# Contracting over 64 features at once in the last query groups of a fused attention and ELU kernel on Trainium2

## The chip, the core and the metric

The kernel runs on one core of a Trainium2 chip. A core has a matrix engine (PE, with its weight loads PEld), a vector engine (DVE), a scalar engine (ACT), a general engine (POOL) and a sync engine (SP) that issues most transfers. [...] The matrix engine can be split into tiles: a matmul of "32*32" uses 32 rows (the contracted features) and 32 columns (the outputs) of the array, so sixteen of them can be placed side by side; of "64*32" eight fit.

The metric is the device time of one execution in microseconds; lower is better. Before the change the median of 3 runs is 262.61 us (262.29 to 262.78).

## The reference

```python
def phi(x):                                   # 32 numbers of a token -> 64 features
    a = einsum('rd,bhsd->bhsr', S1, x); b = einsum('rd,bhsd->bhsr', S2, x)     # r = 8
    return einsum('bhsi,bhsj->bhsij', a, b).reshape(..., 64)
q_p, k_p = phi(q), phi(k)                     # batch 4, heads 4, seq 1088, head_dim 32
kv  = einsum('bhsf,bhsd->bhfd', k_p, v);  z = sum(k_p, axis=2)
num = einsum('bhsf,bhfd->bhsd', q_p, kv)
den = einsum('bhsf,bhf->bhs', q_p, z)[..., None] + 1e-06
x   = (num / den) as 4352 tokens x 128
h   = x @ w_in                                # 128 x 2048
g   = where(h > 0, h, exp(min(h, 0)) - 1)
out = g @ w_out                               # 2048 x 128
```

All arithmetic is float32. S1, S2, w_in and w_out arrive as float64 and are rounded in the kernel from raw word pairs.

## The kernel before

Tokens are cut into half tiles of 64 (`NH` = 68 of them) and these into nine groups: groups 0 to 7 have 512 tokens, group 8 has the last 256, one half tile of 64 for each batch. The feed-forward part runs over groups and over eight pairs of 128-wide slices of the hidden dimension (`cp`). One group with one `cp` is a step; the list `steps` (L970) holds 64 of them, and the loop at L1074 writes the instructions out by hand for each: `mm1` (h from x, `quarters`, L256), the ELU on ACT (`elu_a`, L827 and L829) and DVE (`elu_d`, L835), sums on POOL (`sums7`, L717 to L720) and the second matmul of the step two before (`mm2_seven`, L756). From step 30 on both matmuls use 128*64 tiles. Step 46 is group 5 with `cp` 6, step 62 group 7 with `cp` 6; group 8 is worked off in a tail loop behind them.

The attention part is threaded through these steps with `at`, `mid` and `late`, which name a step and a place in it. For queries, `q1` makes a and b (and the terms of den) for a unit of groups, `q2_den` and `q2_half` divide by den and form the 64 products of each token (`qp`), `q4` turns them in blocks of 32 by 32 on DVE (L651) into `qpT`, and `q5` (L661) multiplies them with kv, giving x for the unit in PSUM; `q5_out` (L672) copies it to SBUF on ACT as `xg`. Units here are 2, 3, (4, 5), (6, 7) and 8. `queries` (L674) runs `q5` of one unit and `q1` of the next in one step, on two `h` banks that the next step's `mm1` uses and two more: step 46 has `q5` of unit 6 (256 columns for each matmul) and `q1` of group 8 (64 columns), step 62 has `q5` of group 8 alone (64 columns).

After `q4`, the 32 rows of one row group w of the array hold one quarter of the unit's tokens (`quarter_of`), 32 of the 64 features at a time: half f=0 and half f=1 lie beside each other in the free dimension. So `q5` is called twice: with f=0 for four heads and four quarters (16 matmuls of 32*32, opening the sums), then `q1` (16 matmuls of 32*32), then f=1 (16 more, closing the sums). The stationary operand is `kvs[b]`: kv of batch b, with 32 features on the partitions, copied to all four row groups. It is written by `KT_out` (L438): DVE turns kv, SP writes it to a DRAM buffer `kvd` (L442) and reads it back four times (once for batch 0) into `kvs` (L445). Units 6 and 7 belong to batch 3; group 8 has one quarter of each batch.

SP works its transfers in order: loads at the start, the copies of `KT_out`, and 16 stores at the end of each group (L804). The raw buffer `raw_2` (L160) of the first two weight slices is not used after their rounding.

Of the kernel before, what the change touches and what calls it, by code (L numbers as in the profile page):

```python
# [12 lines left out]
F32 = mybir.dt.float32  # L13
# [14 lines left out]
def kernel(  # L28
# [21 lines left out]
    nc = tc.nc  # L50
    B, H, S, D = q.shape
    R = S1.shape[0]
    P = 128
# [10 lines left out]
    const = ctx.enter_context(tc.tile_pool(name="const", bufs=1))  # L64
    work = ctx.enter_context(tc.tile_pool(name="wk", bufs=2))
# [75 lines left out]
    wide = S1.dtype != F32  # L141
# [17 lines left out]
    if wide:  # L159
        raw_2 = const.tile([P, 2, 4 * P, 2], U32, name="raw")  # L160
# [163 lines left out]


    kvS = const.tile([P, H, D], F32, name="kvS")
    kvs = {b: const.tile([P, H, 2, D], F32, name=f"kvs{b}") for b in range(B)}
    dram = ctx.enter_context(tc.tile_pool(name="dram", bufs=1, space=bass.MemoryType.DRAM))
    kvd = {b: dram.tile([P, 2 * D], F32, name=f"kvd{b}")[:] for b in range(B)}
    kv_ps, feats, wzs, kf_ps = {}, {}, {}, []  # L330
# [107 lines left out]
    def KT_out(b):  # L438

        kt = work.tile([P, 2 * D], F32, name="kvt", tag="kvt")  # L440
        nc.vector.transpose(kt[:], kv_ps[b][:, :R * R])
        nc.sync.dma_start(kvd[b], kt[:])  # L442
        src = kvd[b].rearrange("(h p) x -> p h x", h=H)
        for w in range(4 if b else 1):
            nc.sync.dma_start(kvs[b][32 * w:32 * w + 32].rearrange("p h f d -> p h (f d)"), src)  # L445

    def ZC(b, ps):
        zl = work.tile([P, H * R], F32, name="zl", tag="zl")
        nc.scalar.copy(zl[:], ps[:, R * R:R * R + H * R])
        return zl  # L450
# [30 lines left out]
    abw, ans, qp, qpT, xg, xps = {}, {}, {}, {}, {}, {}  # L481
# [7 lines left out]
    def half_tile(g, k):  # L489
        return (g // 2, 8 * (g % 2) + k) if g < NQ - 1 else (k, NT - 1)  # L490
# [37 lines left out]
    un = {g: sum(qn[x] for x in gr) for g, gr in units.items()}  # L528

    def quarter_of(g, w):  # L530

        n = un[g] // 2
        return (*half_tile(g + n * w // 8, n * w % 8), n)

    def q1(g, ps, o, opened):
        for w in range(4):
            b, t, n = quarter_of(g, w)
            m, qs = 64 * n, qE[:, b:b + 1, :] if g == NQ - 1 and b < 2 else qT[b][:, t:t + n, :]
            qs = qs.rearrange("p t s -> p (t s)")
            if g == 2:  # L540
                m, qs = 2 * m, _ap(qs, [[8 * 64, 2], [1, m]])
            for r in range(4):
                rows = slice(32 * r, 32 * r + 32)
                nc.tensor.matmul(ps[r][32 * w:32 * w + 32, o:o + m], SWs[rows, b].rearrange("p x r -> p (x r)"),  # L544
                                 qs[rows], start=not opened, stop=True, skip_group_check=True,
                                 tile_position=(32 * r, 32 * w))
        abw[g] = ps, o
# [79 lines left out]
            nc.scalar.copy(to[:, w], xp[w][:, :256].rearrange("p (m s) -> p m s", s=P))  # L627


    def heads(g):  # L630
        return 2 if un[g] > 4 else H

    def q2_a(g, i):
        m = heads(g) * un[g]
        p = psum.tile([P, 512], F32, name="qa", tag="aux")
        ans[g, i] = p[:, :m * R].rearrange("p (m r) -> p m r", r=R)
        nc.scalar.copy(p[:, :m * R], ans[g][:, m * i:m * i + m].rearrange("p m r -> p (m r)"))

    def q2_half(g, i):
        m = heads(g) * un[g]  # L640
        r = slice(m * i, m * i + m)
        qp[g, i] = work.tile([P, 4 * H, R, R], F32, name="qp", tag="qp", bufs=2)
        a_, b_ = ans.pop((g, i)) if (g, i) in ans else ans[g][:, r], abw[g][:, r, :R]
        nc.vector.tensor_mul(qp[g, i][:, :m], _ap(a_, list(a_.ap[1:]) + [[0, R]]),
                             _ap(b_, [b_.ap[1], [0, R], b_.ap[2]]))

    def q4(g, i=0):

        m = heads(g) * un[g]
        qpT[g, i] = work.tile([P, 4 * H, 2, 32], F32, name="qpT", tag="qpT", bufs=2)  # L650
        nc.vector.transpose(qpT[g, i][:, :m].rearrange("p m f s -> p (m f s)"),  # L651
                            qp.pop((g, i))[:, :m].rearrange("p m i j -> p (m i j)"))

    def q5(g, ps, f):
        m4 = un[g]
        for r in range(4):
            i, o = divmod(m4 * r, heads(g) * un[g])
            for w in range(4):
                b, t, n = quarter_of(g, w)
                rows = slice(32 * w, 32 * w + 32)  # L660
                nc.tensor.matmul(ps[w][32 * r:32 * r + 32, :64 * n], kvs[b][rows, r, f, :],  # L661
                                 qpT[g, i][rows, o:o + 2 * n, f, :], start=(f == 0), stop=(f == 1),
                                 skip_group_check=True, tile_position=(32 * w, 32 * r))
        xps[g] = ps

    def q5_out(g, i=0):
# [7 lines left out]
    def queries(g5, g1, n):  # L674

        hs[steps[n]] = [psum.tile([P, 512], F32, name="h", tag="h", bufs=4) for c in range(2)]
        ps = hs[steps[n]] + [psum.tile([P, 512], F32, name="qps", tag="aux") for _ in range(2)]
        if g5 is not None:
            q5(g5, ps, 0)
        if g1 is not None:  # L680
            q1(g1, ps, 256 if g5 is not None else 0, g5 is not None)
        if g5 is not None:
            q5(g5, ps, 1)


# [297 lines left out]
    def late(n, f, *a):  # L983
        extra.setdefault((n, 1), []).append((f, *a))
# [10 lines left out]
    late(2, make_SWs)  # L995
    late(3, Z_share, 0)
    late(3, KT_out, 0)
    zls = {}

    def sums_out(b):  # L1000
        zls[b] = ZC(b, kv_ps[b])
        KT_out(b)
# [32 lines left out]
    for n, g, nx in ((12, None, 2), (15, 2, None), (22, 3, 4), (30, 4, 6), (46, 6, 8), (62, 8, None)):  # L1035
        at(n, queries, g, nx, n + 1)
        if g is not None:
            mid(n, q5_out, g)
        if nx == 2:
            at(n, weights7, slice(NP - 2, NP))  # L1040
            at(n, q1_out_two, (0, 1))
            mid(n, q1_out_two, (2, 3))
        elif nx is not None:
            mid(n, q1_out, nx)
        if g is not None and len(units[g]) > 1:
            late(n, q5_out, g, 1)
    late(12, q2_den, 2)
    late(13, q2_half, 2, 0)
    at(14, q4, 2)
    mid(15, q2_den, 3)  # L1050
    late(19, q2_a, 3, 0)
    late(19, q2_half, 3, 0)
    late(20, q4, 3)
    late(22, q2_den, 4)
    for n, g, i in ((25, 4, 0), (26, 4, 1), (32, 6, 0), (35, 6, 1)):
        late(n, q2_a, g, i)
    at(26, q2_half, 4, 0)
    late(26, q2_half, 4, 1)
    late(27, q4, 4, 0)
    late(28, q4, 4, 1)  # L1060
    late(31, q2_den, 6)
# [1 line left out]
    late(36, q2_half, 6, 1)  # L1063
    late(37, q4, 6, 0)
    late(38, q4, 6, 1)
    late(59, q2_den, 8)
    late(59, q2_half, 8, 0)
    late(60, q4, 8)

    late(15, weights7, slice(0, 3))  # L1070
    late(16, weights7, slice(3, NP - 2))
# [2 lines left out]
    for n in range(2, N):  # L1074
        g, cp = steps[n]
# [29 lines left out]
        g, cp = before  # L1105
# [10 lines left out]
    g = NQ - 2  # L1116
# [53 lines left out]
```

## Time and profile before

| | |
|---|---|
| median of 3 runs | 262.61 us |
| profiled execution: time, span | 262.6 us, 260.5 us |
| PE, DVE, ACT, POOL busy | 255.0, 186.8, 183.2, 158.9 us |
| ordinary step late in the kernel (`mm1` start 183.76 to next 187.00) | 3.24 us |
| step 46 (178.62 to 183.76) | 5.14 us |
| step 62 (232.43 to 236.61) | 4.18 us |
| `q4` of a half of unit 6, of group 8 (L651) | 1.24, 0.70 us |
| q4 of unit 6, start of its two halves | 153.54, 156.78 us |
| q4 of group 8, start | 230.73 us |

Times inside the profile are counted from the start of the span. The time of an execution is its span and some 2 us around it. A line of the timeline merges neighbouring instructions of one kind: start, time to the end of the last, engine, line, what is written from what, the tile ("32*32"), the shape, and how many. Every float32 matmul of the program appears as two (two passes, each with a weight load), so 16 matmuls are 32 lines' worth.

### The profile page before, as it was taken

The numbers are of one execution on the slowest core, as the hardware profiler recorded it, in microseconds if no ns is written. First come the engines' busy times: TensorE is split into PE (matmuls) and PEld (weight loads), VectorE is DVE, ScalarE is ACT, GpSimd is POOL, SyncE is SP. The second block draws the span as 40 slices with busy tenths as digits, with TensorE's granted clock in tenths as the row PEclk, the third lists the DMA queues.
The fourth block names the chain that finished last, engine by engine and source line by source line (L and its number), as shares of the span: only waits on it lengthen the run. The fifth ranks groups of instructions, "written<-read, shape, count | busy, mean of one in ns | idle before, by whom it ended". The sixth has DMA issues, their size and how long they took to land.

```text
span 260.5 us, 9833 instructions
## 1 busy us (share of the span) xinstructions
PE 255.0 (98%) x4187; PEld 158.7 (61%) x4187; DVE 186.8 (72%) x352; ACT 183.2 (70%) x358; POOL 158.9 (61%) x202
## 2 busy tenths in 40 slices
PE   8899999999999999999999999999999999999994
PEld 7652333453346667676666666665666666668994
DVE  6899999999988958997567576743465446674641
ACT  2469878766667577776687777775877777777792
POOL 4420007002279996788678798888588888887410
PEclk9999999999999999999999999999999999999999
DMA  6998089012011210012100200020001100110012
GB/s 172 325 362 223 4 236 263 16 48 67 14 19 28 34 32 13 3 18 36 26 0 4 35 8 3 0 31 12 3 3 29 17 4 0 25 18 3 3 28 38
DMA packets 28507, 14.30 MB, mean 55 GB/s; under 512 B 21392, under 2 KB 26640, under 8 KB 28464
## 3 DMA queue, kind: packets, MB, share of 16 engines
q1 hardware_dynamic: 28032, 13.32, 21.1%
q8 instruction: 33, 0.54, 0.9%
q10 hardware_dynamic: 368, 0.30, 0.3%
q0 software_dynamic: 64, 0.07, 0.1%
q14 instruction: 10, 0.08, 0.1%
HBM read 11.31 MB, written 2.36 MB: 52 GB/s over the span
## 4 chain that ended last, share of the span: by engine, by line
PE 97%; DVE 1%; ACT 0%; issue 0%; DVEq 0%
PE h L256 45%; PE pb L756 17%; PE pa L756 13%; PE o L256 5%; PE pb L732 4%; PE ol L256 3%; PE idle L264 1%; PE kv L432 1%; PE h L661 1%; PE abp L340 1%; PE qps L661 1%; PE h L544 1%; PE qtp L614 1%; DVE qp L602 1%; PE xps L621 0%; PE kfps L362 0%
## 5 line engine op out<-in xcount | busy, mean ns | idle before, releaser
L256 PE MATMUL h<-xg,W 128*32 128x512 f32 (+3 forms) x904 | 130.8, 539 | 0.3 <-ACT xg L627 0.3
L835 DVE SCALAR_TENSOR_TENSOR gg<-e,h 128x512 f32<-128x512 f32 x128 | 86.0, 682 | 53.1 <-ACT e L829 48.7
L827 ACT ACTIVATE e<-h 128x512 f32<-128x512 f32 x128 | 75.5, 590 | 46.4 <-PE h L256 44.5
L829 ACT ACTIVATE e<-e 128x512 f32<-128x512 f32 x128 | 80.9, 632 | 3.8
L717 POOL TENSOR_TENSOR tt<-gg 128x512 f32<-128x512 f32 x50 | 64.2, 1284 | 29.5 <-DVE gg L835 23.7
L256 PEld LDWEIGHTS h<-xg,W 128*32 128x32 f32 (+1 forms) x904 | 43.0, 122 | 42.9 <-issue 34.6
L720 POOL TENSOR_TENSOR tt<-gg,tt 128x256 f32<-128x256 f32 x50 | 36.9, 739 | 3.9
L719 POOL TENSOR_TENSOR tt<-tt,gg 128x256 f32<-128x256 f32 x50 | 36.7, 735 | 3.9
L756 PEld LDWEIGHTS pa<-gg,W 128*64 128x64 f32 (+1 forms) x496 | 23.7, 126 | 22.8 <-issue 22.7
L756 PE MATMUL pa<-gg,W 128*64 128x128 f32 (+1 forms) x496 | 30.6, 274 | 0.0
L756 PE MATMUL pb<-tt,SS 128*64 128x128 f32 (+1 forms) x480 | 29.6, 273 | 0.0
L756 PEld LDWEIGHTS pb<-tt,SS 128*64 128x64 f32 (+1 forms) x480 | 22.8, 126 | 0.0
L756 PE MATMUL pa<-tt,SS 128*32 128x128 f32 (+1 forms) x288 | 21.2, 273 | 0.0
L756 PE MATMUL pb<-tt,W 128*64 128x128 f32 (+1 forms) x256 | 19.9, 273 | 0.0
L756 PE MATMUL pb<-gg,SS 128*64 128x128 f32 (+1 forms) x256 | 19.9, 273 | 0.0
L134 POOL TENSOR_TENSOR raw<-raw,tiny 128x512 f32<-128x512 f32 x1 | 1.0, 1043 | 24.7 <-DVE raw L129 24.7
L256 PE MATMUL o<-gg,W 128*32 128x512 f32 x128 | 15.3, 595 | 0.0
L756 PEld LDWEIGHTS pa<-tt,SS 128*32 128x32 f32 (+1 forms) x288 | 13.7, 124 | 0.0
L756 PEld LDWEIGHTS pb<-tt,W 128*64 128x64 f32 (+1 forms) x256 | 12.8, 125 | 0.0
L756 PEld LDWEIGHTS pb<-gg,SS 128*64 128x64 f32 (+1 forms) x256 | 12.8, 125 | 0.0
L732 PE MATMUL pb<-gg,W 128*32 128x256 f32 x192 | 11.5, 380 | 0.0
L887 DVE SCALAR_TENSOR_TENSOR gg<-e,h 128x256 f32<-128x256 f32 x16 | 6.6, 417 | 6.4 <-PE h L256 3.2
(158 smaller groups left out, 271.3 us busy)
## 6 DMA issues: line engine op xcount, KB each, us to landing
raw<-in_moe_w_in_dram SPq DMA_DIRECT2D x8, 256.0 KB, 6.3
raw<-in_moe_w_out_dram SPq DMA_DIRECT2D x8, 256.0 KB, 6.4
out_dram<-ob SPq DMA_DIRECT2D x112, 16.0 KB, 1.6
hd_k<-in_k_dram SPq DMA_DIRECT2D x3, 544.0 KB, 7.2
hd_q<-in_q_dram SPq DMA_DIRECT2D x3, 544.0 KB, 9.3
v<-in_v_dram SPq DMA_DIRECT2D x4, 288.0 KB, 7.9
v<-in_v_dram SPq DMA_DIRECT2D x4, 256.0 KB, 8.8
kvs<-kvd SPq DMA_DIRECT2D x13, 32.0 KB, 2.7
```

The lines of the kernel that those rows point to most:

```text
L256: nc.tensor.matmul(dst[c:c + tile], lhs[:, c:c + tile], rhs, skip_group_check=True, tile_position=(0, c), **kw)
L264: nc.tensor.matmul(idle[c:c + tile, :cols], ones[:, :tile], ones[:, :cols], skip_group_check=True, tile_position=(0, c))
L661: nc.tensor.matmul(ps[w][32 * r:32 * r + 32, :64 * n], kvs[b][rows, r, f, :], qpT[g, i][rows, o:o + 2 * n, f, :], start=(f == 0), stop=(f ...
L717: nc.gpsimd.tensor_tensor(_ap(t[:, 0], [[4 * P, 2], [P, 2], [1, P]]), _ap(gs[g, cp][:, 0, P:], [[4 * P, 2]] + us), _ap(gs[g, cp][:, 0], [[ ...
L719: nc.gpsimd.tensor_tensor(t[:, 1], t[:, 2], b11, op=ADD)
L720: nc.gpsimd.tensor_tensor(t[:, 3], b21, t[:, 1], op=SUB)
L732: nc.tensor.matmul(acc[1][0][r:r + width[0], 256 * hi:256 * hi + 256], lhs[:, w:w + width[0]], gg[:, c, 256 * u:256 * u + 256], start=(cp ...
L756: nc.tensor.matmul(bank[r:r + width[0], P * col:P * col + P], lhs[:, w:w + width[0]], rhs[:, u], start=(first and i in ((0,) if g == 1 els ...
L827: nc.scalar.activation(e, hs[g, cp][c][:, :n], RELU, scale=-1.0)
L829: nc.scalar.activation(e, e, EXP, scale=-1.0)
L835: nc.vector.scalar_tensor_tensor(gs[g, cp][:, c, :n], es[g, cp][:, c, :n], -1.0, hs[g, cp][c][:, :n], op0=ADD, op1=MAX)
L887: nc.vector.scalar_tensor_tensor(gs["last", k // 2][:, k % 2, :2 * P], es["last", k // 2][:, k % 2, :2 * P], -1.0, hs["last", k][:, :2 * P ...
```

## The change

For units 6 and 8 (`pairs`) the sum over the 64 features is one matmul of 64*32 where it was two of 32*32 that accumulate. Three things are added for that.

`q4` writes its turned blocks with the two halves f apart (`qpF`, f outermost), and then issues 8 transfers on SP that exchange them between row groups: afterwards the 64 rows of a row pair hold all 64 features of one quarter, the even quarters under e=0 and the odd ones under e=1. They go to `exch`, which lies in the old `raw_2` buffer. Unit 6 has two such calls, group 8 one.

`KT_out` writes kv in a second layout `kv2`, with 64 features on the partitions, on the row pairs that need it. `kvs` remains for batches 1 and 2 only.

`q5_pairs` replaces both calls of `q5`: for e=0 and e=1, four heads and two row pairs, 16 matmuls in all, and `q1` follows behind it. Last, the DVE work of group 8 between `q1` and `q5` moves eight steps ahead, from steps 59 and 60 to 51 and 52.

```diff
-    kvs = {b: const.tile([P, H, 2, D], F32, name=f"kvs{b}") for b in range(B)}
+    pairs = (6, 8)
+    pair_b = [g // 2 for g in pairs if g < 8]
+    kvs = {b: const.tile([P, H, 2, D], F32, name=f"kvs{b}") for b in (1, 2)}
+    kv2 = {b: const.tile([P, H, D], F32, name=f"kvp{b}") for b in range(B)}
...
-        for w in range(4 if b else 1):
+        for w in range(4 if b in kvs else 0):
             nc.sync.dma_start(kvs[b][32 * w:32 * w + 32].rearrange("p h f d -> p h (f d)"), src)
+        for u in (0, 1) if b in pair_b else (b // 2,):
+            for f in range(2):
+                r = slice(64 * u + 32 * f, 64 * u + 32 * f + 32)
+                nc.sync.dma_start(kv2[b][r], src[:, :, D * f:D * f + D])
...
+    exch = [raw_2[:, c].bitcast(F32).rearrange("p (e m a) w -> p e m (a w)", e=2, a=16) if wide else
+            const.tile([P, 2, 4 * H, 32], F32, name=f"qpE{c}")[:] for c in range(2)]
...
     def q4(g, i=0):
...
+        t = work.tile([P, 2, 4 * H, 32], F32, name="qpF", tag="qpT", bufs=2)
+        nc.vector.transpose(t[:, :, :m].rearrange("p f m s -> p m f s"),
+                            qp.pop((g, i))[:, :m].rearrange("p m (f i) j -> p m f (i j)", f=2))
+        to = qpT[g, i] = exch[(i + (g > 3)) % 2]
+        for e in range(2):
+            for u in range(0, 4, 2):
+                for f in range(2):
+                    nc.sync.dma_start(to[32 * (u + f):32 * (u + f) + 32, e, :m], t[32 * (u + e):32 * (u + e) + 32, f, :m])
...
+    def q5_pairs(g, ps):
+        for e in range(2):
+            for r in range(4):
+                i, o = divmod(un[g] * r, heads(g) * un[g])
+                for w in (e, e + 2):
+                    b, t, n = quarter_of(g, w)
+                    u = slice(64 * (w // 2), 64 * (w // 2) + 64)
+                    nc.tensor.matmul(ps[w][32 * r:32 * r + 32, :64 * n], kv2[b][u, r, :],
+                                     qpT[g, i][u, e, o:o + 2 * n, :], skip_group_check=True,
+                                     tile_position=(u.start, 32 * r))
+        xps[g] = ps
...
-        if g5 is not None:
+        if g5 in pairs:
+            q5_pairs(g5, ps)
+        elif g5 is not None:
             q5(g5, ps, 0)
         if g1 is not None:
             q1(g1, ps, 256 if g5 is not None else 0, g5 is not None)
-        if g5 is not None:
+        if g5 is not None and g5 not in pairs:
             q5(g5, ps, 1)
...
-    late(59, q2_den, 8)
-    late(59, q2_half, 8, 0)
-    late(60, q4, 8)
+    late(51, q2_den, 8)
+    late(51, q2_half, 8, 0)
+    late(52, q4, 8)
```

More of the change, by code (lines that the diff above doesn't have):

```diff
@@ L649, in q4 @@
         m = heads(g) * un[g]
-        qpT[g, i] = work.tile([P, 4 * H, 2, 32], F32, name="qpT", tag="qpT", bufs=2)
-        nc.vector.transpose(qpT[g, i][:, :m].rearrange("p m f s -> p (m f s)"),
-                            qp.pop((g, i))[:, :m].rearrange("p m i j -> p (m i j)"))
+        if g not in pairs:
+            qpT[g, i] = work.tile([P, 4 * H, 2, 32], F32, name="qpT", tag="qpT", bufs=2)
+            nc.vector.transpose(qpT[g, i][:, :m].rearrange("p m f s -> p (m f s)"),
+                                qp.pop((g, i))[:, :m].rearrange("p m i j -> p (m i j)"))
+            return
+        t = work.tile([P, 2, 4 * H, 32], F32, name="qpF", tag="qpT", bufs=2)
[6 more added lines that the diff above has]
+                    nc.sync.dma_start(to[32 * (u + f):32 * (u + f) + 32, e, :m], t[32 * (u + e):32 * (u + e) + 32, f, :m])
     def q5(g, ps, f):
```

## The prediction

> **What bounds the kernel now.** I read the page first: busy shares and the chain of waits.
>
> ```profile
> PE 255.0 (98%) x4187; PEld 158.7 (61%) x4187; DVE 186.8 (72%) x352; ACT 183.2 (70%) x358; POOL 158.9 (61%) x202
> ...
> PE 97%; DVE 1%; ACT 0%; issue 0%; DVEq 0%
> ```
>
> PE is the bound from end to end: 97% of the chain that ended last is matmul time. So an edit counts by what it does to the time between two matmuls, and DVE, SP and ACT work counts only if it makes PE wait. Then I read the timeline of PE around the two places that the change touches. Step 46:
>
> ```profile
> 178.62 1.89 PE L256 MATMUL h<-xg,W 128*64 128x512 f32 x8
> 180.44 0.41 PE L661 MATMUL h<-qpT,kvs 32*32 32x256 f32 x2
> ...
> 180.90 0.43 PE L544 MATMUL h<-qE,SWs 32*32 32x64 f32 x3
> 181.11 0.25 PE L544 MATMUL qps<-qE,SWs 32*32 32x64 f32 x2
> ...
> 181.34 0.40 PE L661 MATMUL h<-qpT,kvs 32*32 32x256 f32 x1
> ...
> 182.18 0.66 PE L756 MATMUL pa<-gg,W 128*64 128x128 f32 x8
> ...
> 183.76 1.89 PE L256 MATMUL h<-xg,W 128*64 128x512 f32 x8
> ```
>
> and step 62:
>
> ```profile
> 232.43 1.89 PE L256 MATMUL h<-xg,W 128*64 128x512 f32 x8
> ...
> 234.25 0.24 PE L661 MATMUL h<-qpT,kvs 32*32 32x64 f32 x2
> ...
> 234.42 0.22 PE L661 MATMUL qps<-qpT,kvs 32*32 32x64 f32 x2
> 234.51 0.30 PE L661 MATMUL h<-qpT,kvs 32*32 32x64 f32 x3
> ...
> 234.87 0.23 PE L661 MATMUL qps<-qpT,kvs 32*32 32x64 f32 x2
> 235.03 0.66 PE L756 MATMUL pa<-gg,W 128*64 128x128 f32 x8
> ```
>
> Step 46 has three batches of 16 matmuls: f=0 takes 180.90-180.44 = 0.46 us, q1 0.44, f=1 to the next work 0.84; together 1.74. Step 62 has two: 0.26 and 0.52, together 0.78. Everything the change can win on PE lies in these 2.52 us, 1% of the span.
>
> The form that replaces them, 64*32, is in the trace too: step 16 runs two batches of eight such matmuls back to back.
>
> ```profile
> 75.32 0.72 PE L362 MATMUL kfps<-kT,Sxp 64*32 64x288 f32 x16
> 75.83 0.69 PE L362 MATMUL h<-kT,Sxp 64*32 64x288 f32 x16
> 76.45 0.43 PE L756 MATMUL pa<-gg,W 128*32 128x128 f32 x8
> ```
>
> The first batch costs 0.51, the second 0.62 up to the next work in another tile shape.
>
> **The change, part by part.** *The array time does not fall.* Sixteen 32*32 tiles abreast with 256 columns take 0.46; eight 64*32 tiles abreast with 288 take 0.51, and with 256 by the column count (0.51 x 256/288) 0.45 to 0.46. Two batches replace two batches. What halves is the number of matmuls, 32 to 16 for each call. So the gain is in the gaps between batches, and the rows above show these: within q1, 180.90 is followed by 181.11 for the next bank; within step 62, the second batch needs 0.52 where the first needs 0.26 for the same matmuls. The stalls come behind the first 16 matmuls of each attention block. Step 16, with two times eight, shows none.
>
> *Step 46 after.* Two 64*32 batches: 0.46 for the first; for the second with its way out to another shape 0.59, which is what the eight 64*32 matmuls of L621 with 256 columns need, from 20.64 to the next work at 21.23 (step 16's 0.62 with 288 agrees). Sum 1.05. Then q1 alone, 16 matmuls of 64 columns: step 62 prices this from both sides. A first batch needs 234.42-234.25 = 0.17 to its last pair of starts, and from there to the next shape it is 235.03-234.87 = 0.16: 0.33. A second batch needs 0.52. I take 0.33: its matmuls come third, but the sixteen in front stream for 0.9 us, in which they can be queued. 1.05 + 0.33 = 1.38 against 1.74: 0.36 won; with 0.52, 0.17 won; if q1 followed without a gap of its own (0.09 less), 0.45.
>
> *Step 62 after.* Two batches of eight with 64 columns. No row has this. From below: the sixteen matmuls of the first batch and the way out, 0.33. From above: today's 0.78 less the eight matmuls saved in each batch (starts in the first are 0.007 apart, in the second 0.016: 0.05 + 0.13) = 0.60. A weight load takes 0.10 and 64 columns hide only 0.05, so the second batch can't follow as closely as in step 16; I take 0.50. Won 0.28, between 0.18 and 0.45.
>
> [...] The way out of the 64*32 block at 76.45 comes some 0.09 after the last column has streamed. [...]
>
> *Waits on PE.* The built program's list of instructions gives the sixteen matmuls of step 46 22 semaphore waits (most on transfers) where there were 6, and those of step 62 10 where there were 2. One wait rides on the matmul, others need instructions of their own; L432 has such an instruction with two waits, so I count 10 and 4 of them against 2 and 0.
>
> ```profile
> L661 PEldq EVENT_SEMAPHORE  x6: 51/51/51, 68.1 to 178.5; - x6
> ```
>
> Each takes 51 ns, in PE's sequencer. The last is at 178.5, the matmul it belongs to at 180.44: the sequencer runs 1.9 us ahead. 10 x 0.051 = 0.51 and 4 x 0.051 = 0.20 lie under mm1's 1.8 us in front, so I cost them at 0; without that cover they cost up to 0.71. Behind them on PE stand q1 and L756, for which ACT (x to SBUF) and DVE (q1's blocks) wait.
>
> [...]
>
> *Transfers.* 24 exchanges, and 18 kv issues where there were 13: 29 more on SP. L445's four issues take 1.74, 0.43 each; landing 2.7 by the table of transfers. Unit 6: turned at 154.8 and 158.0 (L651, start plus 1.24), 16 x 0.47 = 7.5 us of issues behind stores that began at 145.84, so landed by about 166, 14 us ahead of 180.44. Group 8: its DVE work moves 8 steps x 3.24 = 26 us ahead, so turned at 205.5, eight issues and landing by 212; needed at 234.25. Stores that queue behind have no reader. The one tight place is early: batch 0 gets a second issue (0.47) ahead of the copies for batch 1.
>
> ```profile
> 63.45 1.74 SPq L445 DMA_DIRECT2D kvs<-kvd  x4
> ```
>
> Those land by 65.2+2.7 = 67.9 and are read at 70.75 in step 15; 0.5 later still leaves 2.3. All at 0; with no cover the early issue costs 0.5.
>
> *DVE.* The five operations of q2 for group 8 (0.22, 0.23, 0.20, 0.78, 1.24) and q4 (0.70) go from a step with cp 3 to another with cp 3. At 226.8 to 231.4 they push the ELU's DVE part back and PE keeps its 3.24, so they cost 0 there and here. q4 now writes with a stride; same elements. If it doubled (1.24 to 2.5), DVE's idle 1.47+0.40 in a step would still hold it.
>
> *Sum*: 0.36 + 0.28 = 0.64; bounds 0.17 + 0.18 = 0.35 and 0.45 + 0.45 = 0.90. The profiled execution is 262.6 (span 260.5 and 2.1 around it), the median 262.61, so I subtract from the median: 261.97, between 261.7 and 262.25.
>
> **Rivals.** *A, the gaps stay*: the stalls belong to the count of batches (three and two, as now), not of matmuls. Then only the low bounds are won, 0.35: 262.25. For it: array time is equal. Against: the two batches of step 16.
>
> *B, slower: the waits empty the queue.* If a wait is only passed when the matmuls in front have gone, each of the 8 + 4 matmuls with waits on transfers (step 46: heads 0 and 2 of both batches; step 62: head 0 of both) restarts the flow. Price: the restart 180.90 to 181.11 less the normal distance, about 0.18, twelve times, 2.2, plus 0.71 for the instructions, less 0.64: 2.3 slower, 264.9. At 0.24 each it decides from the fifth restart on (1.2 against 0.64 + 0.53). For it: 14 such instructions in a stretch of 1.4 us. Against: the one at 178.5.
>
> *C, more*: in both steps the first eight L756 take 0.66 where others take 0.61, and start late; if the shorter block lets their weights be loaded ahead, 0.15 more in each step: 0.64 + 0.30 = 0.94, 261.65.
>
> **Chances.** Forecast 0.70, A 0.10, B 0.13, C 0.07. What this kernel's measurement can tell from no change is about 0.2%, 0.53 us: the forecast's centre lies just outside, its low part inside; I give 0.56 of its 0.70 to faster and 0.14 to no difference. Faster 0.56 + 0.07 = 0.63, the same 0.14 + 0.10 = 0.24, slower 0.13. The range takes in A and C and the 0.15 that runs lie around their median, and of B only the edge: 261.4 to 262.7.
>
> **What would show it.** Step 46 should take 5.14-0.36 = 4.8, step 62 4.18-0.28 = 3.9, all other steps 3.24; the 64*32 batches start 0.46 apart in step 46; the semaphore instructions of step 46 lie before 180.4. I am wrong if q1 starts more than 1.1 after the first 64*32 matmul, if PE waits for a transfer in these steps, or if a step that the change does not touch grows.

## The result, and the profile after

| | before | after |
|---|---|---|
| median of 20 runs each | 262.44 us (262.13 to 264.43) | 261.93 us (261.73 to 263.27) |
| step 46, `mm1` to the next `mm1` | 5.14 us | 4.86 us |
| step 62 | 4.18 us | 3.92 us |

The ratio after to before is 0.9983, 95% interval 0.9975 to 0.999. Run again later beside an experiment, the changed kernel gave 261.94 us (11 runs) against 262.43 (15 runs), again 0.9983 (0.9974 to 0.9992). So it is faster, by 0.51 us. That is 0.19%, just below the 0.2% that the prediction had named as what a measurement tells from no change; with twenty runs of each kernel the interval lies below 1 all the same.

The shares of the page after and the chain of waits read as before: PE is the bound from end to end.

```profile
span 260.6 us, 9756 instructions
...
PE 254.8 (98%) x4123; PEld 158.4 (61%) x4123; DVE 186.9 (72%) x352; ACT 183.4 (70%) x358; POOL 159.0 (61%) x202
...
PE 97%; DVE 1%; ACT 0%; issue 0%; DVEq 0%
```

PE has 64 matmul records fewer: 16 float32 matmuls in each of the two steps, two records to a matmul. Its busy time falls by 0.2 us only, because batches overlap and a gap between two starts lies under records that still run (in step 62 a gap of 0.11 us under records of 0.21 to 0.24). The length of a step says more. The timeline of PE after, step 46 (columns as before: start, time to the end of the last, engine, line, operation, names, tile, shape, count):

```profile
178.98 1.89 PE L256 MATMUL h<-xg,W 128*64 128x512 f32 x8
180.80 0.40 PE L693 MATMUL h<-raw,kvp 64*32 64x256 f32 x1
...
181.25 0.38 PE L693 MATMUL h<-raw,kvp 64*32 64x256 f32 x1
...
181.56 0.38 PE L693 MATMUL qps<-raw,kvp 64*32 64x256 f32 x1
181.87 0.24 PE L551 MATMUL h<-qE,SWs 32*32 32x64 f32 x2
...
182.25 0.66 PE L790 MATMUL pa<-gg,W 128*64 128x128 f32 x8
...
183.83 1.89 PE L256 MATMUL h<-xg,W 128*64 128x512 f32 x8
```

The block of step 46 is 182.25 - 180.80 = 1.45 (1.74 before): 0.45 for the first 64\*32 batch, 0.62 for the second with its way out, 0.38 for q1. Step 62 after:

```profile
232.50 1.89 PE L256 MATMUL h<-xg,W 128*64 128x512 f32 x8
234.32 0.24 PE L693 MATMUL h<-raw,kvp 64*32 64x64 f32 x1
...
234.46 0.27 PE L693 MATMUL h<-raw,kvp 64*32 64x64 f32 x2
234.57 0.21 PE L693 MATMUL qps<-raw,kvp 64*32 64x64 f32 x1
...
234.70 0.22 PE L693 MATMUL qps<-raw,kvp 64*32 64x64 f32 x1
234.84 0.66 PE L790 MATMUL pa<-gg,W 128*64 128x128 f32 x8
...
236.42 1.03 PE L256 MATMUL h<-xg,W 128*64 128x512 f32 x4
```

Its block is 0.52 (0.78 before), with a hole of 0.11 between 234.46 and 234.57. All other steps have their old length to 0.006 us. So 0.28 + 0.26 = 0.54 us were won on PE, and the timed medians show 0.51 of it.

The two profiled spans alone would mislead: 260.5 before, 260.6 after. The rows show why. `mm1` of step 46 stands at 178.98 after and 178.62 before, 0.36 later, although every step from 16 us on up to it is the same. The start of that execution was longer, and such starts differed by some 0.5 us between the profiled executions of this study (0.28 later in waits_first, 0.14 earlier in three_units3, against before). Steps, not spans, are compared below.

The transfers that the change added, in the timeline of SP after:

```profile
155.16 10.78 SPq L672 DMA_DIRECT2D raw<-qpF  x16
...
205.70 4.95 SPq L672 DMA_DIRECT2D raw<-qpF  x8
```

The issues are dearer than predicted, 10.78/16 = 0.67 each where 0.47 was taken, but they end at 165.9 and 210.7, 15 and 24 us ahead of their readers; from issue to landing such a transfer takes 1.8 to 3.9 us, and neither step waits for one.

### The profile page after: what moved, and what is told of

It is laid out like the page before. It is cut to its first block, busy times and chain, and to the rows that moved or that the text cites. A ratio compares the mean times of both kernels' runs of the same rounds, so it can differ in the third digit from the quotient of the medians.

```text
span 260.6 us, 9756 instructions
## 1 busy us (share of the span) xinstructions
PE 254.8 (98%) x4123; PEld 158.4 (61%) x4123; DVE 186.9 (72%) x352; ACT 183.4 (70%) x358; POOL 159.0 (61%) x202
## 4 chain that ended last, share of the span: by engine, by line
PE 97%; DVE 1%; ACT 0%; issue 0%; DVEq 0%
PE h L256 45%; PE pb L790 17%; PE pa L790 13%; PE o L256 5%; PE pb L766 4%; PE ol L256 3%; PE idle L264 1%; PE kv L435 1%; PE abp L343 1%; PE h L681 1%; PE h L551 1%; PE qtp L621 1%; DVE qp L609 1%; PE h L693 1%; PE xps L628 0%; PE kfps L365 0%
## 5 line engine op out<-in xcount | busy, mean ns | idle before, releaser
L790 PEld LDWEIGHTS pa<-gg,W 128*64 128x64 f32 (+1 forms) x496 | 23.7, 126 | 22.4 <-issue 22.2
L790 PE MATMUL pa<-gg,W 128*64 128x128 f32 (+1 forms) x496 | 30.6, 274 | 0.0
L790 PE MATMUL pb<-tt,SS 128*64 128x128 f32 (+1 forms) x480 | 29.6, 273 | 0.0
L790 PEld LDWEIGHTS pb<-tt,SS 128*64 128x64 f32 (+1 forms) x480 | 22.8, 126 | 0.0
L790 PE MATMUL pa<-tt,SS 128*32 128x128 f32 (+1 forms) x288 | 21.2, 273 | 0.0
L790 PE MATMUL pb<-gg,SS 128*64 128x128 f32 (+1 forms) x256 | 19.9, 273 | 0.0
L790 PE MATMUL pb<-tt,W 128*64 128x128 f32 (+1 forms) x256 | 19.9, 273 | 0.0
L790 PEld LDWEIGHTS pa<-tt,SS 128*32 128x32 f32 (+1 forms) x288 | 13.7, 124 | 0.0
L790 PEld LDWEIGHTS pb<-gg,SS 128*64 128x64 f32 (+1 forms) x256 | 12.8, 125 | 0.0
L790 PEld LDWEIGHTS pb<-tt,W 128*64 128x64 f32 (+1 forms) x256 | 12.8, 125 | 0.0
```

Source lines behind the costliest of these rows:

```text
L790: nc.tensor.matmul(bank[r:r + width[0], P * col:P * col + P], lhs[:, w:w + width[0]], rhs[:, u], start=(first and i in ((0,) if g == 1 els ...
```

## The experiments

Eleven runs were made, one of them the changed kernel again. Times are medians; the kernel before, run beside them, gave 262.40 to 262.53. Lengths of steps are differences of `mm1` starts in one profiled execution; the changed kernel's second profile gave 4.86 and 3.92 for steps 46 and 62 once more. The four kernels named three_units have the order of waits_first as well.

| kernel | step 30 | step 31 | step 46 | step 62 | time, us |
|---|---|---|---|---|---|
| before | 5.51 | 3.24 | 5.14 | 4.18 | 262.44 |
| after | 5.51 | 3.24 | 4.86 | 3.92 | 261.93 |
| q1_last | 5.51 | 3.24 | 5.14 | 4.18 | 262.41 (one run) |
| same_tile | 5.51 | 3.24 | 5.26 | 3.83 | 262.17 (one run) |
| q1_mid | 5.51 | 3.24 | 5.24 | 3.93 | 262.25 (one run) |
| q1_first | 5.51 | 3.24 | 5.31 | 3.92 | 262.75 (one run) |
| waits_first | 5.51 | 3.24 | 4.86 | 3.78 | 261.81 |
| late | 5.51 | 3.24 | 4.86 | 9.13 | 267.11 (one run) |
| three_units | 3.45 | 9.12 | 4.86 | 3.78 | 265.18 |
| three_units2 | 4.31 | 5.20 | 4.86 | 3.78 | 264.11 |
| three_units3 | 3.45 | 5.20 | 4.86 | 3.78 | 261.51 |
| three_units4 | 3.25 | 5.25 | 4.86 | 3.78 | 261.62 |

### Is it the place of q1, or the new form?

In step 46 the change does two things: the sums get another form, and q1 comes behind them instead of between. q1_last does only the second, in the kernel before.

```diff
         if g5 is not None:
             q5(g5, ps, 0)
+        if g5 is not None and g5 >= 6:
+            q5(g5, ps, 1)
         if g1 is not None:
             q1(g1, ps, 256 if g5 is not None else 0, g5 is not None)
-        if g5 is not None:
+        if g5 is not None and g5 < 6:
             q5(g5, ps, 1)
```

> The kernel before, in 32*32 tiles, with q1 of group 8 moved behind both halves of q5 in step 46, the order that the changed kernel has. Theory: the stall comes behind the first sixteen matmuls of a block however they are ordered, and 48 matmuls remain; step 46 stays near 5.14 (5.05 to 5.15). Rival: the gain of step 46 comes from the order (one long run of equal matmuls, q1's small ones at the end), not from the 64*32 form: step 46 falls to about 4.86 as in the changed kernel. Step 62 stays at 4.18 in both.

Step 46 took 5.14, as before. In the old form the place of q1 gives nothing; the gain is the new form's. The timeline of PE of q1_last behind the first sixteen matmuls:

```profile
180.83 0.59 PE L661 MATMUL h<-qpT,kvs 32*32 32x256 f32 x2
181.04 0.40 PE L661 MATMUL qps<-qpT,kvs 32*32 32x256 f32 x1
```

Here f=1, which adds to the sums of f=0, comes next and stalls for 0.21 us. In the kernel before, q1 comes next, writes other columns, and stalls as long (180.90 to 181.11). So the stall does not come from adding to an open sum. A kernel with half as many matmuls in 32\*32 tiles was not run: whether the count of the matmuls or their shape is what helps is not told apart.

### Which half of the form: fewer matmuls, or the turn over the tiles?

same_tile keeps the 64\*32 matmuls and puts the two of one tile directly behind each other.

```diff
-        for e in range(2):
-            for r in range(4):
-                i, o = divmod(un[g] * r, heads(g) * un[g])
-                for w in (e, e + 2):
+        for r in range(4):
+            i, o = divmod(un[g] * r, heads(g) * un[g])
+            for w in (0, 1, 2, 3):
+                e = w % 2
...
```

> The changed kernel with the 64x32 matmuls of one tile (even heads, then odd heads, of the same row pair) directly behind each other, instead of eight tiles in turn. [...]

Two outcomes had been set against each other: about 7 us for step 46 (8 tiles x 0.43 = 3.4 for the pairs instead of 1.07) and 4.7 to 5.6 for step 62, or 4.86 and 3.92 as in the changed kernel. Both were wrong. The timeline of PE of same_tile in step 46:

```profile
180.30 0.40 PE L694 MATMUL h<-raw,kvp 64*32 64x256 f32 x1
...
181.53 0.38 PE L694 MATMUL qps<-raw,kvp 64*32 64x256 f32 x1
181.83 0.24 PE L551 MATMUL h<-qE,SWs 32*32 32x64 f32 x2
...
182.16 0.66 PE L791 MATMUL pa<-gg,W 128*64 128x128 f32 x8
```

The sixteen matmuls take 181.83 - 180.30 = 1.53 against 1.07 in turn, far from 3.4, and step 46 is longer than in the kernel before (5.26 against 5.14). How much of that is the turn is not shown: four of the ten wait instructions of step 46 fall into the block here as well, at other places (180.3 to 180.7), so the turn is worth 0.40 there at most. Step 62 shows its price alone, for there all four waits are met ahead of the block, which starts at 234.24 (the view is explained under the waits, below):

```profile
L694 PEldq EVENT_SEMAPHORE  x4: 51/51/51, 231.8 to 233.6; - x4
```

The kernel to compare with is waits_first, below, whose waits are ahead there too: 3.83 against 3.78, so with 64 columns the turn is worth 0.05. That 3.83 is less than the 3.92 of the changed kernel is no merit of the order; the changed kernel meets two waits inside the block. One more row counts later: q1 takes 182.16 - 181.83 = 0.33 here.

### What does a change of shape cost?

q1_mid puts q1 between the two 64\*32 batches, one change of shape more.

```diff
         if g5 in pairs:
-            q5_pairs(g5, ps)
+            q5_pairs(g5, ps, (0,) if g1 is not None else (0, 1))
...
+        if g5 in pairs and g1 is not None:
+            q5_pairs(g5, ps, (1,))
```

> The changed kernel, with q1 of group 8 between the two batches of eight in step 46 instead of behind them; step 62 is not touched. This puts a change of tile shape more into step 46 (64*32, 32*32, 64*32, then 128*64) and changes nothing else in the work. [...] Rival: the change of shape costs nothing by itself, the 0.09 is the end of the block and comes once: 4.86 as it was.

The timeline of PE of q1_mid, the first start of each batch and the next work:

```profile
180.31 0.40 PE L693 MATMUL h<-raw,kvp 64*32 64x256 f32 x1
...
180.90 0.24 PE L551 MATMUL h<-qE,SWs 32*32 32x64 f32 x2
...
181.33 0.40 PE L693 MATMUL h<-raw,kvp 64*32 64x256 f32 x1
...
182.14 0.66 PE L792 MATMUL pa<-gg,W 128*64 128x128 f32 x8
```

0.59 + 0.43 + 0.81 = 1.83 against 0.45 + 0.62 + 0.38 = 1.45 after. Followed by another shape the first batch needs 0.14 more than followed by its own kind (0.59 against 0.45); the rest lies in q1 (0.05) and in the second batch (0.19). Whether that 0.19 is the change of shape alone is not shown: in this second batch matmuls start at 181.35, 181.45 and 181.58, 0.10 to 0.13 apart, much as the late waits of the changed kernel do (below). The direction was expected, the size not: step 46 took 5.24, 0.38 more, where 4.95 to 5.05, 0.1 to 0.2 more, was expected.

### Where are the waits met?

The prediction costed the fourteen wait instructions on PE at nothing, since the sequencer ran ahead. The trace after, PE's sequencer at the line of the new matmuls, in four stretches of time (how many, shortest/median/longest in ns, first and last start):

```profile
L693 PEldq EVENT_SEMAPHORE  x6: 51/51/51, 178.3 to 179.3; - x6
...
L693 PEldq EVENT_SEMAPHORE  x4: 51/51/51, 180.8 to 181.2; - x4
...
L693 PEldq EVENT_SEMAPHORE  x2: 51/51/51, 231.9 to 232.4; - x2
...
L693 PEldq EVENT_SEMAPHORE  x2: 51/51/51, 234.3 to 234.5; - x2
```

Those of the first batches are met some 2 us ahead (1.5 to 2.5). Those of the second batches come up only when the block has begun (180.80 and 234.32), four in 0.39 us, 0.13 apart. Two experiments bear on this. waits_first takes even and odd heads in turn by row of tiles, so that the matmuls with waits come in the first batch:

```diff
-        for e in range(2):
+        for k in range(2):
             for r in range(4):
+                e = (r + k) % 2
```

> The changed kernel, with the 16 matmuls of q5_pairs in another order: in the first batch of eight the heads 0 and 2 take e=0 and the heads 1 and 3 take e=1, in the second batch the other way round. So every exchanged region and every kv copy is touched by the first eight matmuls, and no wait on a transfer is left in the second batch; matmuls, shapes and transfers are the same. In the changed kernel's trace the wait instructions of the first batch are done about 2 us ahead, those of the second batch only from 180.82 and 234.34 on, about 0.126 us apart, while the batch should start. Theory: these are what the second batch lacks: step 46 falls from 4.86 to about 4.80 (0.05 less), step 62 from 3.92 to about 3.83 (0.09 less), every other step stays at 3.24; 0.14 us in all, 0.05% of the time, which the timing itself will hardly tell. Rival: the waits are hidden there too and the second batch is slow for its weight loads: step 46 and step 62 stay at 4.86 and 3.92. Second rival: eight waiting matmuls in a row in front can't be passed in the 2 us of lead: step 46 grows by up to 0.3.

q1_first puts q1 in front, so that its sixteen matmuls stand ahead of all ten waits of step 46:

```diff
-        if g5 in pairs:
-            q5_pairs(g5, ps)
-        elif g5 is not None:
+        if g5 is not None and g5 not in pairs:
             q5(g5, ps, 0)
         if g1 is not None:
...
+        if g5 in pairs:
+            q5_pairs(g5, ps)
```

> The changed kernel with q1 of group 8 ahead of the 64x32 matmuls in step 46, still one change of shape each way. [...]

The same view of waits_first has nine of the ten at or before 180.3 in step 46 and the tenth at 180.4, where its block starts at 180.72, and all four of step 62 by 233.4:

```profile
L694 PEldq EVENT_SEMAPHORE  x9: 51/51/51, 178.3 to 180.3; - x9
...
L694 PEldq EVENT_SEMAPHORE  x4: 51/51/51, 231.8 to 233.4; - x4
```

The timeline of its PE in step 62, first and last matmul of the block and the next work:

```profile
234.25 0.24 PE L694 MATMUL h<-raw,kvp 64*32 64x64 f32 x1
...
234.49 0.22 PE L694 MATMUL qps<-raw,kvp 64*32 64x64 f32 x1
234.63 0.66 PE L791 MATMUL pa<-gg,W 128*64 128x128 f32 x8
```

The hole is gone (block 0.38, was 0.52): the two late waits had cost 0.14. That the new order of the matmuls won it is unlikely: same_tile has yet another order, its waits are ahead too, and its block has no hole either (0.43). In waits_first, step 46 stayed at 4.86: the second batch runs without holes (0.57 instead of 0.62), but q1 then takes 0.43 instead of 0.38.

In q1_first all ten are met inside the block, and the matmuls come apart:

```profile
L693 PEldq EVENT_SEMAPHORE  x10: 51/51/51, 180.9 to 182.0; - x10
```

The timeline of PE there (the first rows of q1, then the first and last of the 64\*32 matmuls):

```profile
180.74 0.24 PE L551 MATMUL h<-qE,SWs 32*32 32x64 f32 x2
...
181.07 0.61 PE L693 MATMUL h<-raw,kvp 64*32 64x256 f32 x2
...
182.34 0.38 PE L693 MATMUL qps<-raw,kvp 64*32 64x256 f32 x1
182.65 0.66 PE L790 MATMUL pa<-gg,W 128*64 128x128 f32 x8
```

1.91 in all: q1 0.33 and the sixteen matmuls 1.58, where they need 1.07 in the changed kernel. The transfers had landed some 10 us before (the issues end at 165.9 in the changed kernel, and a landing takes 3.9 at most), and PE has no idle time there that a wait ended. So waits that were already satisfied still had a price where the sequencer met them inside the block. The ten come 0.12 to 0.13 apart, but part of that lies under matmuls that run: together they cost 0.51, 0.05 each. The two in step 62 of the changed kernel cost 0.07 each, the four in its step 46, met while the first batch runs, 0.05 together. Met ahead, as all four in step 62 of waits_first, they show no price (its block of 0.38 has no hole). For step 46 of q1_first 5.1 to 5.2 was expected, or 4.75 to 4.9 if the waits were passed ahead there too; measured was 5.31.

### Is the cover of the exchange needed?

late puts the DVE work of group 8 back to where the kernel before had it.

```diff
-    late(51, q2_den, 8)
-    late(51, q2_half, 8, 0)
-    late(52, q4, 8)
+    late(59, q2_den, 8)
+    late(59, q2_half, 8, 0)
+    late(60, q4, 8)
```

> The changed kernel with the denominators, products and transpose of group 8 back in steps 59, 59 and 60, where the kernel before had them. Theory (the exchange is free only because it was started eight steps earlier): the transpose ends at about 231.5, eight exchanges issued at 0.5-0.6 each and some 2 us to the landing of the last end at 237.5-238.5, where the block of step 62 starts at 234.3: step 62 grows by 3.2-4.2 us, the time to 265-266, and PE waits there for a DMA. Rival: the exchange is quick enough from step 60 too, the move of the DVE work was not needed: 261.9.

The timeline of PE of late (in brackets the idle time in front and who ended it):

```profile
233.88 0.30 PE L693 MATMUL h<-raw,kvp 64*32 64x64 f32 x2
234.93 0.21 PE L693 MATMUL qps<-raw,kvp 64*32 64x64 f32 x1 [0.76 <-DMA raw<-qpF]
...
236.21 0.27 PE L693 MATMUL h<-raw,kvp 64*32 64x64 f32 x2 [0.94 <-DMA raw<-qpF]
237.87 0.28 PE L693 MATMUL qps<-raw,kvp 64*32 64x64 f32 x1 [1.39 <-DMA raw<-qpF]
...
238.26 1.12 PE L790 MATMUL pa<-gg,W 128*64 128x128 f32 x8
...
241.19 1.88 PE L256 MATMUL h<-xg,W 128*64 128x512 f32 x8
```

The exchange is over at 237.9, where it was expected, and PE waits 0.76 + 0.94 + 1.39 = 3.09 us for it. The step grew by 5.21 over the changed kernel's, a good 1 us more than the 3.2 to 4.2 expected. The block accounts for 3.86 (238.26 - 233.88 = 4.38 against 0.52): the 3.09 in which no matmul ran, and 0.77 more for the matmuls, which ran in small groups between the waits. The rest is the work behind it, 241.19 - 238.26 = 2.93 against 1.58. It ran at a lower clock, as the table of stretches shows (length, busy time of each engine, granted clock, DMA share, GB/s):

```profile
234.00:238.20 4.20, 1.11 (x32) 0.61 (x31) 0.69 (x1) 0.61 (x2) 2.11 (x3) 0.94 0.17 41
238.20:241.20 3.00, 3.00 (x41) 2.94 (x31) 0.69 (x1) 1.57 (x5) 0.40 (x1) 0.52 0.02 5
```

For 3 us after the wait the granted clock was 0.52; in the stretch behind it, 241.2 to 244.4, it was 1.00 again. In three_units, below, PE also waited 2.09 us out of 4.6 and the clock stayed at 1.00; what makes the difference is not shown. The early exchange is not a refinement of this change: without it the kernel loses ten times what the new form wins.

### The same form for group 4: four tries

The block of groups 4 and 5 is the largest left in the old form. Its exchange has little room: the second product of DVE is ready late. three_units moves the block one step on and its DVE work forward:

```diff
-    pairs = (6, 8)
+    pairs = (4, 6, 8)
...
-    for n, g, nx in ((12, None, 2), (15, 2, None), (22, 3, 4), (30, 4, 6), (46, 6, 8), (62, 8, None)):
+    for n, g, nx in ((12, None, 2), (15, 2, None), (22, 3, 4), (31, 4, 6), (46, 6, 8), (62, 8, None)):
...
-    late(26, q2_half, 4, 1)
-    late(27, q4, 4, 0)
-    late(28, q4, 4, 1)
+    late(26, q4, 4, 0)
+    late(27, q2_half, 4, 1)
+    at(28, q4, 4, 1)
+    late(29, stores7, 2)
```

> The order of waits_first, and the 64*32 form for unit (4, 5) too (pairs 4, 6, 8). For that its q5 goes from step 30 to 31, its two q4 to steps 26 and 28, and the stores of group 2 behind them on SP (step 29). Theory: step 30 falls to 3.24 and step 31 takes over its block with 0.3 to 0.5 less than before (step 30 had 5.50, so step 31 has 5.0 to 5.2): about 0.4 us less than waits_first in all, 0.95 less than the kernel before, ratio to it about 0.9965. Rival: the exchange of unit 4 is late (its last eight transfers are issued some 9 us ahead of the matmuls and need about 5 us of issues and 2 us of landing): then PE waits at the start of step 31's block by the missing part, up to 3 us. Second rival: x of group 4 reaches step 32 only one step after its sums, so that step 32 starts later by up to 0.7.

It was slower, ratio 1.0099 (1.0063 to 1.0135). The timeline of SP shows whom the last eight exchanges stood behind:

```profile
116.61 6.06 SPq L672 DMA_DIRECT2D raw<-qpF  x8
122.77 0.53 SPq L445 DMA_DIRECT2D kvd<-kvt  x1
124.44 2.81 SPq L452 DMA_DIRECT2D kvp<-kvd  x4
127.35 4.96 SPq L672 DMA_DIRECT2D raw<-qpF  x8
```

The transfers of the keys of batch 3 came first in the queue, and one of them waits for the landing of another (122.77 to 124.44). They were issued until 132.3, where the block began at 129.74, and PE waited three times for them, 2.09 in all. That counts only the time with no matmul at all: from 130.03 to 133.87 six matmul records ran, and these 3.84 us are nearly all of the 3.92 by which step 31 is longer than in three_units2, where nothing is late. three_units2 defers these transfers (`KT_copy`, called by `late(29, KT_copy, 3)`) and puts four of the last eight exchanges on ACT's queue:

```diff
+        if b < 3:
+            KT_copy(b)
...
+                    eng = nc.scalar if (g, i) == (4, 1) and f else nc.sync
```

> As three_units (group 4 and 5 by the 64x32 form too, moved from step 30 to 31; passes in turn as in waits_first), but the transfers of the keys of batch 3, which stood ahead of the last eight exchanges on SP, are put behind them, and four of those eight go out on ACT's queue. Theory (three_units lost 3.8 us only because the exchange was issued too late): it lands by 128.5-129, ahead of the block at 129.7; step 31 about 5.0, steps 30 and 31 together 0.3-0.4 below the changed kernel's; about 0.9955-0.996 of the kernel before, 0.4 us less than waits_first. Rivals: the exchange is late still and PE waits for a DMA in step 31 (264-265); or ACT's four issues at 0.55 each hold up the ELU, and steps 28 to 30 grow by some 0.5-2 us.

PE no longer waited for a transfer, yet the ratio was 1.0066 (1.0052 to 1.008). The timeline of ACT:

```profile
117.38 0.17 ACT L461 COPY zl<-kv 128x32 f32<-128x32 f32 x1
121.15 2.67 ACTq L678 DMA_DIRECT2D raw<-qpF  x4
123.86 0.60 ACT L874 ACTIVATE e<-h 128x512 f32<-128x512 f32 x1 [6.31 <-DMA raw<-qpF]
```

ACT stood 3.6 us for DVE's transpose and issued for 2.67, so the ELU behind them had 6.3 us without work in front of it: step 29 grew by 1.82, step 30 was 0.86 longer than in three_units. three_units3 sends only two exchanges over ACT, each behind ELU work that is due before:

```diff
+                    rest.append((to[32 * (u + f):32 * (u + f) + 32, e, :m], t[32 * (u + e):32 * (u + e) + 32, f, :m]))
+                    if (g, i) != (4, 1) or not (e and u):
+                        nc.sync.dma_start(*rest.pop())
...
+    late(28, q4_rest)
+    mid(29, q4_rest)
```

> As three_units2, but only two of the last eight exchanges go out on ACT's queue, one behind the ELU of step 28 and one between the ELU's halves of step 29, well behind the transpose (121.1), so that ACT doesn't stand and wait for it; the other fourteen on SP at about 0.71 each, 116.4 to 126.3. Theory (three_units2 lost only what ACT lost: it stood 3.6 us for the transpose and issued for 2.7): the last exchange lands by 128.4, the block of step 31 starts at about 129.9, no wait for a DMA; steps 28 to 31 together 0.25-0.35 below the changed kernel's; 261.4-261.6 us, about 0.996 of the kernel before. Rival: an issue on ACT costs PE time wherever it stands (0.67 each, ELU slack gone): steps 29 and 30 grow by 0.3-1.3, 262-263 us.

> The changed kernel unaltered, on the same chip beside three_units3: about 261.9 us, 0.998 of the kernel before; theory of three_units3: 0.3-0.5 us slower than it; its rival: as fast or faster.

three_units3 took 261.51 us (261.49 to 261.57, 5 runs), ratio to before 0.9966 (0.9953 to 0.9978); the changed kernel on the same chip 261.94 (261.84 to 262.37). The ranges do not overlap: this version beats both. Of the 0.43 the steps explain 0.24: 0.14 in step 62 (the waits), 0.10 in steps 30 and 31. That 0.10 is less than the 0.25 to 0.35 expected, because step 30, now without a block, takes 3.45 instead of 3.24: the other matmuls turn there from 32-column to 64-column tiles, and that change of shape used to fall on the block's own. three_units4 moves it to step 31 (`if n == 31: width[0] = 64`).

> As three_units3, with the turn of the other matmuls from 32-column to 64-column tiles one step later (31 instead of 30), so that it falls on the block's own change of shape. Theory: alone in step 30 that turn costs what step 30 of three_units3 shows over a plain step, 3.45 against 3.25, about 0.2; beside the block's it costs nothing: step 30 of 3.25, step 31 as before at 5.19, 0.2 less in all, 261.3 us, 0.996 of the kernel before. Rival: the turn of 0.2 goes along to step 31 (5.3-5.4), no gain: 261.5.

Step 30 fell to 3.25, step 31 rose to 5.25: 0.15 less in all. The time, 261.62 us (261.30 to 261.94), ratio 0.9965 (0.9951 to 0.9979), can't be told from three_units3's.

## Why the prediction came out as it did

**The mechanism held.** The prediction placed the gain in the gaps that half as many matmuls leave out, not in the place of q1 or in array time. q1_last shows that the place gives nothing; the first 64\*32 batch took 0.45 (predicted 0.46), so array time did not fall. Where it fell short is that it named the number of matmuls alone. In step 62 the new form with its half as many matmuls is enough: the three orders that were run (3.92, 3.83, 3.78) all stay below the 4.18 of before. In step 46 it is not: same_tile has the same number and loses all of the gain. The order of the matmuls, which the prediction took for granted with its row from step 16, is a part of the gain there, by the turn over the tiles or by where the waits fall; the runs do not separate these two.

**The sizes.** Step 46 was to win 0.36 and won 0.28. The second batch with its way out took 0.62 for 0.59, q1 0.38 for 0.33. Step 62 was to win 0.28 and won 0.26, its block 0.52 for 0.50. The sum was 0.54 for 0.64, well inside its bounds of 0.35 and 0.90, and the time 261.93 for 261.97; that the two times are closer than the sums is luck: the median of before moved from 262.61 with 3 runs to 262.44 with 20. (Rival C's 261.65 is 261.67 by its own terms, 262.61 - 0.94.)

**The step that failed: "Each takes 51 ns, in PE's sequencer ... 10 x 0.051 = 0.51 and 4 x 0.051 = 0.20 lie under mm1's 1.8 us in front, so I cost them at 0."** The cover held for eight of the fourteen. The sequencer was 2 us ahead for the first batch and not at all for the second. The price in step 62 is shown: 0.14 (waits_first; same_tile, with its waits ahead, has no hole either). The 0.50 predicted there thus came out nearly right because two misses cancel: with its waits covered the block is 0.38, close to the lower bound of 0.33; the argument that 64 columns can't hide a weight load, which raised it to 0.50, is contradicted by that block, whose 32 records start 0.04 or less apart from first to last, with weight loads of 0.102 to 0.107. In step 46 removing the late waits gave 0.05 in the batch and lost 0.05 in q1.

**q1 at 0.33 for want of a row.** The prediction reasoned that q1 can be queued while the sixteen matmuls in front stream for 0.9 us. same_tile and q1_first show q1 at exactly 0.33, with 1.53 us of the block's matmuls in front, or the whole of `mm1`. With 1.07 in front it is 0.38, and 0.43 behind waits_first's smoother batches (1.03). So q1 was at 0.33 where more stood in front of it, and dearer where less did; why, no run shows.

**The rivals.** A (gaps stay, 0.35 won) lies below the 0.54 measured. B (each wait restarts the flow, 2.3 slower) is refuted, its mechanism too: the late waits of the changed kernel are passed at 180.8 to 181.2, while the first batch, begun at 180.80, still runs. What exists is a smaller price of waits met in the block: in q1_first the ten of them lengthen the step by 0.45 over the changed kernel's, far from 2.3. C (the work behind the block, L790, starts quicker) did not occur: its first eight still take 0.66.

**The price of a change of shape.** The prediction took 0.09 for the way out of a 64\*32 block, its estimate from the end of step 16's block. (The rows of step 16 give 0.11, 0.62 less 0.51.) The runs show 0.14 in q1_mid at the way out of the first batch, and 0.15 less in three_units4, where two changes of shape fall together, than in three_units3.

**The transfers and DVE at 0** held, by the margins above; late prices the cover, at 5.2 us. `q4` with its stride still takes 1.24 for a half of unit 6. Of the signs named as fatal none occurred: q1 started 1.07 after the first 64\*32 matmul (bound 1.1), PE waited for no transfer, no untouched step grew. The sign "the semaphore instructions of step 46 lie before 180.4" came out wrong for four of ten.

**Open.** Why q1 and the second batch trade 0.05 for 0.05 in step 46 is argued from the spacing of starts, not shown. The reason for the stalls behind the first sixteen matmuls (0.21 us in q1_last) and for the late waits is not shown, and the number of matmuls and their 64-row shape were changed together. What the turn over the tiles alone is worth with 256 columns is not known. Of the 0.43 between the changed kernel and three_units3, 0.19 is not in the steps; the start of the profiled executions differs by more than that.

## What to carry to other kernels

When PE is the bound, compare the start of one fixed instruction from step to step, and price a block by its batches: half as many matmuls for the same array time saved gaps here (0.28 and 0.26 us). Let consecutive matmuls go to different tiles: not doing so cost 0.05 where the waits were covered, and with waits inside the block the whole gain was lost. Count where PE's wait instructions fall: those of the matmuls that come first in a block were covered by the work in front (met 1.5 to 2.5 us ahead), those behind eight or sixteen other matmuls of the block were not. Putting the operands that need waits first won 0.14 in step 62 and nothing in step 46. Before a value is routed over transfers, find every queue that the issues stand in: one issue behind a landing, or on the engine whose next work PE awaits, cost more here (3.92 us in step 31 of three_units, 1.82 in step 29 of three_units2) than such a form can win.

## What the hardware did that was not expected

- Satisfied waits on PE's sequencer, 51 ns long, came 0.12 to 0.13 us apart when met inside a block (four in 0.39 us after; ten from 180.9 to 182.0 in q1_first), and cost 0.05 to 0.07 us each (0.51 for ten in q1_first, 0.14 for two in step 62), less under a running batch (0.05 for four in step 46) and nothing that shows when met ahead (step 62 of waits_first, block of 0.38 without a hole).
- Two 64\*32 matmuls of one tile directly behind each other hold back the others by little: sixteen took 0.43 us instead of 0.38 with 64 columns, and 1.53 instead of 1.07 with 256, there with four waits in the block, where 3.4 was one of the two expectations.
- After PE's waits in late (3.09 us within 4.2) the granted clock was 0.52 for some 3 us, and the work behind the block took 2.93 us instead of 1.58.
- An exchange of 64 KB cost 0.67 us to issue on SP in a row of sixteen, and one of 32 KB 0.62 in a row of eight; the four issues of kvs, also 32 KB each, took 0.43 each in the kernel before.
